# Second-layer weight blocks decoded at other places, kept in device memory in between, in a spectral convolution with two gated MLPs

## The chip, the cores and the metric

The kernel runs on one core of one Trainium2 chip. The metric is the device time of one execution in microseconds (us), the median of several runs. The profiled execution is one more execution, taken with the hardware profiler.

## What is computed

Activations, two filter arrays and five weight arrays come in; the weights are double precision. A spectral convolution over 3008 positions (2 batches, 256 channels) is followed by two MLPs over the 6016 tokens that result. Cut to what matters:

```python
def _attn_ref(x, filt_r, filt_i):              # x: (2, 3008, 256)
    X = np.fft.rfft(x, axis=1)
    Y = X * (filt_r + 1j * filt_i)[None]
    return np.fft.irfft(Y, n=x.shape[1], axis=1)

def _moe_ref(x, w_gate, w_val, w_out):         # 256 -> 1536 -> 256
    gate = 1.0 / (1.0 + np.exp(-(x @ w_gate)))
    return gate * (x @ w_val) @ w_out

def _moe2_ref(x, w_in, w_out):                 # 256 -> 2048 -> 256
    h = x @ w_in
    return h * (1.0 / (1.0 + np.exp(-1.702 * h))) @ w_out
```

## The kernel before

**Precision.** Every operand of TensorE is a pair of float32 tiles, a high part (rounded by a ScalarE copy) and a low part (the rest, a subtraction on VectorE or GpSimd). `mm3` (L119) makes one product out of three matmuls, high by high, high by low and low by high (L120, L121, L122). The weights arrive as double-precision bits, in blocks of 128 x 512 values. One block is decoded on VectorE and ScalarE: two mask operations, three combining ones, a high copy, a low subtraction. For the first layer this is `decode_steps` (L152), for the second `decode_chores` (L1048).

**Stages.** The tokens are in 12 tiles of up to 512 (the last two of each batch have 480). First comes the convolution of batch 0 (to about 65 us of the trace). Then a first pass of the first MLP layer over tiles 0 to 3 (`s12`, to 187 us) runs while the first layer's 18 weight blocks are decoded, about three for every two steps `f` of the hidden dimension (12 steps of 128). Then the convolution of batch 1 runs interleaved with tiles 2 to 5 (187 to 390 us). Up to here, from the end of the first convolution, the order of instructions on PE, DVE, ACT and POOL is left to the framework; SP's queue follows the program's order throughout.

From about 400 us on, the order on all engines is the program's. Tiles 6 to 11 go in pairs (`for p in range(3, nt // 2)`), and each hidden step of a pair is computed with **seven products instead of eight** (a Strassen-like scheme): `Forms` (L838 to L890) makes the sums and differences of the two input halves, with a high and a low part each, and `combine_w1` those of the weights. The second layer does the same for six pairs of tiles, 8 double steps `fp` each (`for p in range(nt // 2)`); one `fp` is 7 products and 8 back products (`Block.back`) of three matmuls, 45 matmuls.

**Chores.** Work that is not on the way of a step is put into a list of small steps (`chores`), each a few instructions. `spend(q, n)` takes `n` of them at fixed places in each hidden step, and when the list is empty it takes the next second-layer weight block from `bulk`. A block with an odd number (from `w_out`) has 5 steps: `start`, `mant`, `sign`, `value`, `low`. One with an even number (from `w_in`) has 8, since it also makes the sums of its sub-blocks (`sums`, L1092 to L1103). Between two takings the step's own instructions stand: in the second layer L1405 (`y = x + s5`), L1407 (`z = z + s1`) and L1414 (`w = x + s5`) on DVE, the gate (L1334, L1335) twice for each of the four results on ACT, and its low part (L1338) on POOL. TensorE's product 6 overwrites what L1405 reads, so it waits for it.

**Where second-layer weights lie.** There are 16 blocks, two for each `fp`. Blocks 0 to 3 lie in `wl`, 4 to 15 in `wg`, over the first layer's weights, which is why block 4 can't be decoded before the last first-layer pair has passed its step. Before: blocks 0 to 3 are decoded beside pair 4, 4 to 6 beside pair 5, and 7 to 15 beside the first second-layer pair, with 10 chores for each `fp` (`rate = (3, 1, 3, 3)`). `raw_job` loads the next block's bits, `next_raw` those of the first layer's, into `raw` tiles of the `st0`, `st1`, `st3` and later `st2` pools; `slots` lists the free ones.

Of the kernel before, what the change touches and what calls it, by code (L numbers as in the profile page):

```python
# [17 lines left out]
P = 128  # L18
S = 3008
B = 2  # L20
D = 256
# [66 lines left out]
def kernel(  # L88
# [23 lines left out]
    xscr = dram.tile([12, D, 512], F32, name="xscr")  # L112

# [85 lines left out]

    def next_raw():  # L200
        if jobs and slots:
            load_raw(jobs.pop(0))
# [711 lines left out]
    for t in range(2, 6):  # L914
        for f in range(FK if t < 4 else 0, FC1):
# [30 lines left out]
            if pools is not None and k == NCH + 3:  # L946
# [16 lines left out]
                sp = [w34.tile([P, 6, P], F32R, name=f"sp{i}") for i in range(2)]  # L963
# [9 lines left out]
                fs.dst[3] = [packed(w, n) for w in xk]  # L973
# [7 lines left out]
                w2, w3 = lazy(lambda: combos(PRE)), lazy(lambda: combos(PRE + 1))  # L981
                pre = [w2]
                pre += [lambda: (fs.hi(0), fs.hi(1)), lambda: (fs.lo(0), one(), fs.hi(4)), lambda: fs.lo(1)]
                pre += [lambda: (fs.lo(4), two(), fs.hi(5)), lambda: (three(), fs.lo(5)), four]
                pre += [lambda: fs.hi(3), lambda: fs.lo(3), w3]
# [26 lines left out]
    fs.dst[2], fs.dst[6] = ([packed(h[:, c], n) for h in k26] for c in range(2))  # L1012


    NJ = FC2
    KEEP = NWL

    def slot(j):
        if j < KEEP:
            return [w[:, j] for w in wl]  # L1020
        return [w[:, j - KEEP].rearrange("p v c m -> p (v c m)") for w in wg]

    jobs2 = []
    for i in range(0, FC2, 2):
        jobs2.append((rows(w_in2[:, i * P:(i + 2) * P]), 2 * P))
        jobs2.append((rows(w_out2[i * P:(i + 2) * P, :]), D))
# [6 lines left out]
    def spare3(fp):  # L1033
        if fp < 2:
            return [x[:, 3 * fp:3 * fp + 3, :] for x in sp]
        if fp < 6:
            a = 0 if fp < 4 else 8
            b = 3 * (fp % 2)
            return [w[:, a:a + 4, :].rearrange("p f (c m) -> p (f c) m", c=2)[:, b:b + 3, :] for w in wo]
        return [x[:, 24 + 3 * (fp - 6):27 + 3 * (fp - 6), :] for x in sx1]  # L1040

    def spare2(i):
        return [x[:, i % 3, :] for x in spare3(i // 3)]

    def decode_chores(j):
        fp = j // 2
        hi, lo = slot(j)
        sp = spare3(fp)  # L1048
        t = {}

        def start():
            t["raw"], _, _, own = raws.pop(0)
            slots.append(own)
            t["lw"], t["hw"] = t["raw"][:, :, 0], t["raw"][:, :, 1]
            ex = st.tile([P, 512], U32, tag="ex", name="ex")
            nc.vector.tensor_single_scalar(ex, t["hw"], 0x7FF00000, op=ALU.bitwise_and)  # L1056
            t["c"] = st.tile([P, 512], I32, tag="c", name="c")
            nc.scalar.activation(out=t["c"], in_=ex, func=AF.Relu, bias=ebias, scale=8.0)
            t["m"] = st.tile([P, 512], U32, tag="m", name="m")
            nc.vector.tensor_scalar(t["m"], t["hw"], 0xFFFFF, 0x100000, op0=ALU.bitwise_and, op1=ALU.bitwise_or)  # L1060

        def mant():
            t["f"] = t["m"].bitcast(F32)
            nc.vector.scalar_tensor_tensor(  # L1064
                out=t["f"], in0=t["lw"], scalar=2.0**-32, in1=t["m"], op0=ALU.mult, op1=ALU.add
            )

        def sign():
            cu = t["c"].bitcast(U32)
            nc.vector.scalar_tensor_tensor(  # L1070
                out=cu, in0=t["hw"], scalar=0x80000000, in1=cu, op0=ALU.bitwise_and, op1=ALU.bitwise_or
            )
            raw_job(j + 2)

        def value():
            nc.vector.scalar_tensor_tensor(  # L1076
                out=t["f"], in0=t["f"], scalar=2.0**-20, in1=t["c"].bitcast(F32), op0=ALU.mult, op1=ALU.mult
            )
            nc.scalar.activation(out=hi, in_=t["f"], func=AF.Copy)

        def low():
            nc.vector.tensor_sub(lo, t["f"], hi.bitcast(F32))  # L1082
            if j % 2:
                done.add(j)

        def sums(k):
            if k == 0:
                t["v"] = t["f"].rearrange("p (c i m) -> p c i m", c=2, m=P)
                t["r"] = st.tile([P, 4, P], F32, tag="ex", name="wr")
            v, r = t["v"], t["r"]  # L1090
            if k == 0:
                nc.vector.tensor_add(r[:, 0], v[:, 0, 1], v[:, 1, 1])  # L1092
                nc.vector.tensor_sub(r[:, 1], r[:, 0], v[:, 0, 0])
            else:
                nc.vector.tensor_sub(r[:, 2], v[:, 0, 0], v[:, 0, 1])
                nc.vector.tensor_sub(r[:, 3], v[:, 1, 0], r[:, 1])
                nc.scalar.activation(out=hi[:, P:2 * P], in_=r[:, 0], func=AF.Copy)
                nc.scalar.activation(out=sp[0], in_=r[:, 1:], func=AF.Copy)

        def end():  # L1100
            r = t["r"]
            nc.vector.tensor_sub(lo[:, P:2 * P], r[:, 0], hi[:, P:2 * P].bitcast(F32))
            nc.vector.tensor_sub(sp[1], r[:, 1:], sp[0].bitcast(F32))  # L1103
            done.add(j)

        return [start, mant, sign, value] + ([low] if j % 2 else [lambda: sums(0), low, lambda: sums(1), end])

    done = set()
# [13 lines left out]
    def forms_chores(dst, n, raws, spread, split_too):  # L1122
        def make():
            fs = Forms(dst, n, raws, spread, [st.tile([P, 512], F32, tag=k, name="xs") for k in ("ex", "c", "m")])
            cell.append(fs)
            steps = fs.sums()
            if split_too:
                ks = (0, 1, 4, 5, 2, 6, 3)
                steps.append(lambda: fs.hi(0))
                for k, nxt in zip(ks, ks[1:]):  # L1130
                    steps += [lambda k=nxt: fs.hi(k), lambda k=k: fs.lo(k)]
                steps.append(lambda: fs.lo(3))
            return steps

        cell = []
        return lazy(make), cell
# [43 lines left out]

    left = None
    held = []
    low2 = None
    ready = set(range(PRE + 2))
# [11 lines left out]
    for p in range(3, nt // 2):  # L1196
        n = tiles[2 * p][3]
        rhs = [[h[:, :n] for h in d] for d in setA]
        for f in range(FC1):
# [12 lines left out]
            if first_set:  # L1212
                chores += [lazy(lambda q=q: weights(q)) for q in range(PRE + 2, FC1)]
# [5 lines left out]
            if p + 1 < nt // 2:  # L1219
                if f == 9:  # L1220
                    lz, cell = forms_chores(setA, tiles[2 * p + 2][3], raw2, True, False)
                    chores.append(lz)
            elif f == 7:
                lz, cell = forms_chores(setB, 512, raw2, False, True)
                chores.append(lz)
            if p == 3 and f == 10:
                raw_job(0)
                raw_job(1)
            if f == 0:
                bulk += range(4) if p == 4 else ()  # L1230
            if p == 5 and f == 3:
                bulk += range(4, 7)
            rate = {3: (1, 2, 1), 4: (1, 2, 0), 5: (1, 2, 1)}[p]
            if p == 4 and f > 8 or p == 5 and f < 3:
                rate = (0, 0, 0) if not chores else rate
# [10 lines left out]
            if first_set:  # L1246
                fs.hi(6)
                fs.hi(2)
# [14 lines left out]
            if first_set:  # L1263
                fs.lo(6)
# [14 lines left out]
            if first_set:  # L1279
                fs.lo(2)  # L1280
# [5 lines left out]
            if last:  # L1286
                nf.hi(6)
                nf.lo(1, nc.gpsimd)
                nf.lo(6)
# [3 lines left out]
            if last:  # L1293
# [15 lines left out]
            if last:  # L1309

                def low2(nf=nf):
                    nf.hi(3)
                    nf.lo(2)
# [12 lines left out]
    class Block:  # L1326
        def __init__(self, i, j, p, fp, bank):
            self.i, self.j, self.t, self.fp, self.bank = i, j, 2 * p + j, fp, bank
            self.n = tiles[self.t][3]

        def act(self):
            self.gp = [x[:, :self.n] for x in gslot()]
            self.sg = work.tile([P, 512], F32, tag="sg", name="sg")[:, :self.n]
# [3 lines left out]
        def low(self):  # L1337
            nc.gpsimd.tensor_sub(self.gp[1], self.sg, self.gp[0].bitcast(F32))  # L1338
# [21 lines left out]

    for p in range(nt // 2):
# [3 lines left out]
        for fp in range(FC2 // 2):  # L1365
# [4 lines left out]
            if fp == 0:  # L1370
                bulk += range(7, NJ) if p == 0 else ()
                while p and chores:
                    chore(chores)
            while 2 * fp + 1 not in done:
                spend(chores, 1)
# [7 lines left out]
            if not asked and (fp >= 3 if p else fp >= 4 and not bulk and not chores or fp == 6):  # L1383
                asked = True
                lz, cell = forms_chores(setA if p % 2 == 0 else setB, tiles[2 * p + 2][3], raw2, False, True)
                chores.append(lz)
            rate = (2, 0, 1, 1) if p else (3, 1, 3, 3) if fp else (0, 0, 0, 3)
# [6 lines left out]
            if left:  # L1394
                for step in left:
                    step()
                left = None
            back()
# [4 lines left out]
            spend(chores, rate[0])  # L1403
# [5 lines left out]
            bz.low()  # L1409
            back()  # L1410
            back()
            spend(chores, rate[1])
            prod(x, 6, False)
            nc.vector.tensor_add(w, x, s5[:, :n])  # L1414
# [59 lines left out]
```

## Time and profile before

| | us |
|---|---|
| median of 3 runs | 1184.28 (1182.04 to 1185.79) |
| the profiled execution's own time | 1183.55 |
| its span, first to last instruction | 1181.7 |
| PE busy in the span | 1149.4 (97%) |
| DVE busy | 696.4 (59%) |
| ACT busy | 674.7 (57%) |
| POOL busy | 480.3 (41%) |

A matmul of 128 x 512 takes about 0.39 us by its record, but the next one starts 0.227 us after it; 20 us in which TensorE never waits hold 90 of them. So the count of matmuls in a stretch tells more than the busy share.

### The profile page before, as it was taken

The numbers are of one execution on the slowest core, as the hardware profiler recorded it, in microseconds if no ns is written. First come the engines' busy times: TensorE is split into PE (matmuls) and PEld (weight loads), VectorE is DVE, ScalarE is ACT, GpSimd is POOL, SyncE is SP. The second block draws the span as 40 slices with busy tenths as digits, with TensorE's granted clock in tenths as the row PEclk, the third lists the DMA queues.
The fourth block names the chain that finished last, engine by engine and source line by source line (L and its number), as shares of the span: only waits on it lengthen the run. The fifth ranks groups of instructions, "written<-read, shape, count | busy, mean of one in ns | idle before, by whom it ended". The sixth has DMA issues, their size and how long they took to land.

```text
span 1181.7 us, 14171 instructions
## 1 busy us (share of the span) xinstructions
PE 1149.4 (97%) x4994; PEld 933.3 (79%) x4994; DVE 696.4 (59%) x1149; ACT 674.7 (57%) x1274; POOL 480.3 (41%) x385
## 2 busy tenths in 40 slices
PE   8999999999999899999999988899999999999998
PEld 4468888888888788788888866788888888888887
DVE  6899965465564877877778799843333323233211
ACT  5656644665653555655555655566556556556554
POOL 3910104666663211211211244455555555545443
PEclk9999999999999999999999999899999999999999
DMA  8565502232302200012012033020020100200000
GB/s 199 154 189 176 128 1 75 61 92 67 94 14 81 69 21 1 25 48 72 1 54 72 1 96 101 1 72 1 1 72 1 48 22 1 72 1 1 36 1 34
DMA packets 36007, 66.51 MB, mean 56 GB/s; under 512 B 3648, under 2 KB 12480, under 8 KB 35936
## 3 DMA queue, kind: packets, MB, share of 16 engines
q1 hardware_dynamic: 33968, 62.45, 18.0%
q10 hardware_dynamic: 1968, 3.17, 0.8%
q8 instruction: 39, 0.64, 0.2%
q14 instruction: 32, 0.26, 0.1%
HBM read 45.02 MB, written 19.79 MB: 55 GB/s over the span
## 4 chain that ended last, share of the span: by engine, by line
PE 81%; DVE 10%; DMA 3%; ACT 3%; issue 2%; POOL 1%; SPq 0%; ACTq 0%; DVEq 0%; POOLq 0%
PE ps L120 27%; PE ps L121 27%; PE ps L122 27%; DMA f<-in_fd_dram 2%; DVE c L1070 1%; DVE ex L1056 1%; DVE wg L1082 1%; POOL y L341 1%; DVE m L1076 1%; DVE yp L843 1%; DVE m L1064 1%; DMA yraw<-yscr 0%; POOL v L337 0%; DMA yraw<-tt 0%; DVE m L1060 0%
## 5 line engine op out<-in xcount | busy, mean ns | idle before, releaser
L1338 POOL TENSOR_TENSOR g<-sg,g 128x512 fp32r<-128x512 f32 (+1 forms) x128 | 169.4, 1338 | 168.7 <-ACT sg L1335 163.1
L117 POOL TENSOR_TENSOR g<-sg,g 128x512 fp32r<-128x512 f32 (+1 forms) x80 | 102.2, 1277 | 311.3 <-ACT g L116 297.9
L120 PE MATMUL ps<-yp,wg 128*128 128x512 f32 (+1 forms) x442 | 171.9, 389 | 1.0 <-ACT wg L177 0.8
L121 PE MATMUL ps<-yp,wg 128*128 128x512 f32 (+1 forms) x442 | 170.9, 387 | 0.8 <-DVE yp L117 0.8
L122 PE MATMUL ps<-yp,wg 128*128 128x512 f32 (+1 forms) x442 | 170.4, 386 | 0.0
L1405 DVE TENSOR_TENSOR ps<-ps,tabs 128x512 f32<-128x512 f32 (+1 forms) x48 | 33.0, 688 | 198.8 <-PE ps L122 198.7
L1334 ACT ACTIVATE g<-ps 128x512 fp32r<-128x512 f32 (+1 forms) x128 | 75.9, 593 | 85.8 <-DVE ps L1407 58.0
L1338 POOL TENSOR_TENSOR wo<-sg,wo 128x512 fp32r<-128x512 f32 (+1 forms) x64 | 85.8, 1352 | 78.6 <-ACT sg L1335 74.7
L1335 ACT ACTIVATE sg<-ps 128x512 f32<-128x512 f32 (+1 forms) x192 | 114.1, 594 | 3.3 <-POOL g L1338 1.8
L120 PE MATMUL ps<-g,wo 128*128 128x512 f32 (+1 forms) x288 | 111.3, 386 | 0.4 <-ACT wo L177 0.4
L121 PE MATMUL ps<-g,wo 128*128 128x512 f32 (+1 forms) x288 | 111.3, 386 | 0.4 <-POOL g L117 0.4
L122 PE MATMUL ps<-g,wo 128*128 128x512 f32 (+1 forms) x288 | 111.0, 386 | 0.0
L120 PEld LDWEIGHTS ps<-yp,wg 128*128 128x128 f32 x442 | 83.0, 188 | 18.3 <-ACT wg L177 1.2
L121 PEld LDWEIGHTS ps<-yp,wg 128*128 128x128 f32 x442 | 83.0, 188 | 16.6 <-issue 1.7
L122 PEld LDWEIGHTS ps<-yp,wg 128*128 128x128 f32 x442 | 82.9, 188 | 16.0
L116 ACT ACTIVATE g<-sg 128x512 fp32r<-128x512 f32 (+1 forms) x80 | 49.6, 620 | 55.7 <-DVE sg L464 30.4
L120 PE MATMUL ps<-g,wg 128*128 128x512 f32 (+1 forms) x192 | 74.0, 386 | 0.0
L122 PE MATMUL ps<-g,wg 128*128 128x512 f32 (+1 forms) x192 | 74.0, 386 | 0.0
L121 PE MATMUL ps<-g,wg 128*128 128x512 f32 (+1 forms) x192 | 74.0, 386 | 0.0
L1414 DVE TENSOR_TENSOR ps<-ps,tabs 128x512 f32<-128x512 f32 (+1 forms) x48 | 33.0, 688 | 56.5 <-PE ps L122 56.5
L120 PEld LDWEIGHTS ps<-g,wo 128*128 128x128 f32 x288 | 54.1, 188 | 11.9 <-ACT wo L177 0.8
L1334 ACT ACTIVATE wo<-ps 128x512 fp32r<-128x512 f32 (+1 forms) x64 | 38.0, 594 | 44.4 <-DVE ps L1407 31.1
(290 smaller groups left out, 2770.6 us busy)
## 6 DMA issues: line engine op xcount, KB each, us to landing
yraw<-xscr SPq DMA_DIRECT2D x16, 512.0 KB, 4.4
raw<-in_w_out_dram SPq DMA_DIRECT2D x14, 512.0 KB, 3.9
x<-in_xd_dram SPq DMA_DIRECT2D x15, 384.0 KB, 5.3
yraw<-yscr SPq DMA_DIRECT2D x11, 512.0 KB, 5.3
yscr<-tt SPq DMA_DIRECT2D x40, 128.0 KB, 2.1
xscr<-yraw SPq DMA_DIRECT2D x10, 512.0 KB, 2.8
f<-in_fd_dram SPq DMA_DIRECT2D x23, 192.0 KB, 4.4
raw<-in_w_in_dram SPq DMA_DIRECT2D x8, 512.0 KB, 3.8
```

What stands on the lines that cost most here:

```text
L116: nc.scalar.activation(out=dst_hi, in_=src, func=AF.Copy)
L117: lo_eng.tensor_sub(dst_lo, src, dst_hi.bitcast(F32))
L120: nc.tensor.matmul(out=o, lhsT=w[0], rhs=x[0], start=first, stop=False, **kw)
L121: nc.tensor.matmul(out=o, lhsT=w[0], rhs=x[1], start=False, stop=False, **kw)
L122: nc.tensor.matmul(out=o, lhsT=w[1], rhs=x[0], start=False, stop=last, **kw)
L341: eng.tensor_add(y, y, v)
L843: (eng or nc.vector).tensor_sub(self.dst[k][1], self.src[k], self.dst[k][0].bitcast(F32))
L1334: nc.scalar.activation(out=self.gp[0], in_=self.bank, func=AF.Gelu_apprx_sigmoid)
L1335: nc.scalar.activation(out=self.sg, in_=self.bank, func=AF.Gelu_apprx_sigmoid)
L1338: nc.gpsimd.tensor_sub(self.gp[1], self.sg, self.gp[0].bitcast(F32))
L1405: nc.vector.tensor_add(y, x, s5[:, :n])
L1414: nc.vector.tensor_add(w, x, s5[:, :n])
```

## The change

It does the following.

- Blocks 0 to 3 are appended to `jobs`, so that their bits are loaded and decoded in the first pass (`decode_next`), behind the first layer's 18 blocks. Their high and low parts go into one place, tiles of `st1` (`early_place`), and from there to a new tensor in device memory (`wscr`; the sums to `sscr`). `st1` gets no more raw bits from then on.
- Blocks 4 to 15 are in `bulk` from the start of pair 4; blocks 4 to 11 are decoded into `wl` in turn (`j % NWL`) and stored to `wscr`, 12 to 15 stay there. Blocks below 12 are loaded into `wg[j]` (`reload`) once the last first-layer pair has passed step j; the sums are loaded by `reload_s` into `wo`, `sx0` and `sx1`.
- The numbers of chores taken change: `RATE` and the lines behind it for the first layer, with `hold_back` at the end of pairs 4 and 5; `(0, 0, 0)` for the first `fp` and `(3, 2, 2)` for the others of the first second-layer pair, at three places instead of four. `spend` stops ahead of a `low` or `end` step unless it is the first that it takes.
- Two inputs of the first-layer pairs (numbers 2 and 6) get tiles of their own (`ks`, `kr`), so that some high and low copies are made earlier instead of in the pair's first or last step. `w3` is combined inside pair 3.
- In the first `fp` of the first second-layer pair, the first block keeps its gate result in PSUM and makes its low part on DVE, one place later (`own`).

The core of the diff:

```diff
+    wscr = dram.tile([FC1, 2, P, 512], F32, name="wscr")
+    sscr = dram.tile([FC2 // 2 - 1, 2, P, 3 * P], F32, name="sscr")
...
+        def spill():
+            done.add(j)
+            if j < KEEP:
+                for i, x in enumerate((hi, lo)):
+                    nc.sync.dma_start(out=wscr[j, i], in_=x.bitcast(F32))
+            if j % 2 == 0 and fp < 7:
+                for i, x in enumerate(sp):
+                    nc.sync.dma_start(out=sscr[fp, i], in_=x.rearrange("p k m -> p (k m)").bitcast(F32))
...
+    KEEP = FC1
+    EARLY = 4
+    jobs += [(j, [jobs2[j][0]], jobs2[j][1]) for j in range(EARLY)]
+
+    def early_place():
+        own = stage[1]
+        w = own.tile([P, 2, 512], F32R, tag="raw", name="wl0")
+        return [w[:, 0], w[:, 1]] + [own.tile([P, 3, P], F32R, tag=k, name="sp0") for k in ("c", "m")]
...
             if raws and (t == 0 or f % 2 == 1):
-                decode(nc.vector)
+                decode_next()
                 next_raw()
     while raws:
-        decode(nc.vector)
+        decode_next()
...
+                kr = st2.tile([P, 2, 512], F32R, tag="raw", name="kr", bufs=2)
+                fs.dst[2], fs.dst[3], fs.dst[6] = ([packed(w, n) for w in k] for k in (ks, xk, kr))
...
+    def reload(j):
+        placed.add(j)
+        for i, x in enumerate(slot(j)):
+            nc.sync.dma_start(out=x.bitcast(F32), in_=wscr[j, i])
...
+    RATE = {3: (1, 2, 2), 4: (1, 2, 1), 5: (1, 2, 1)}
+    SPARE = (4, 0), (5, 1), (11, 5)
...
     def spend(q, n):
-        for _ in range(n):
-            if not q and bulk:
-                q.extend(decode_chores(bulk.pop(0)))
+        for k in range(n):
+            if not q and bulk and not hold_back:
+                q.extend(next_decode(bulk.pop(0)))
+            if k and q and getattr(q[0], "apart", False):
+                return
             chore(q)
...
+                raw_job(EARLY)
+            if p == 4 and f == 0:
+                raw_job(EARLY + 1)
+                bulk += range(EARLY, NJ)
+            hold_back = p == 4 and f > 7 or p == 5 and f > 6
+            rate = RATE[p] if p == 3 or f > 2 else (0, 2, 1) if f else (0, 0, 1)
+            if p == 5:
+                for q in range(FC1):
+                    if q < f and q in done and q not in placed:
+                        reload(q)
+                for q, g in SPARE:
+                    if f >= q and 2 * g in done and g not in summed:
+                        reload_s(g)
...
+            if p == 0:
+                for g in (0, 1, 4, 5, 6, 2, 3):
+                    if (fp or g not in (2, 3)) and 2 * g in done and g not in summed:
+                        reload_s(g)
+                for q in range(FC1):
+                    if q in done and q not in placed:
+                        reload(q)
+                while 2 * fp + 1 not in done:
+                    spend(chores, 1)
...
-            rate = (2, 0, 1, 1) if p else (3, 1, 3, 3) if fp else (0, 0, 0, 3)
+            rate = (2, 1, 1) if p else (3, 2, 2) if fp else (0, 0, 0)
```

## Rows read from the trace of the kernel before

**Rows 1.** The page: span, busy time by engine, PE in 40 slices.

```profile
span 1181.7 us, 14171 instructions
...
PE 1149.4 (97%) x4994; PEld 933.3 (79%) x4994; DVE 696.4 (59%) x1149; ACT 674.7 (57%) x1274; POOL 480.3 (41%) x385
...
PE   8999999999999899999999988899999999999998
```

**Rows 2.** Windows (stretch, busy by engine, granted clock, DMA): second-layer pairs 0, 1.

```profile
674.00:775.00 101.00, 88.31 (x355) 68.42 (x354) 89.19 (x118) 61.42 (x117) 48.32 (x34) 0.95 0.18 58
774.00:856.00 82.00, 82.00 (x363) 67.94 (x362) 26.27 (x39) 47.60 (x89) 42.30 (x32) 1.00 0.08 26
```

**Rows 3.** Timeline of DVE (start, duration): L1405 of second-layer pairs 0, 1, 2.

```profile
674.51 0.69 DVE L1405 TENSOR_TENSOR ps<-ps,tabs 128x512 f32<-128x512 f32 x1
...
774.30 0.70 DVE L1405 TENSOR_TENSOR ps<-ps,tabs 128x512 f32<-128x512 f32 x1
...
776.95 0.70 DVE L1414 TENSOR_TENSOR ps<-ps,tabs 128x512 f32<-128x512 f32 x1 [1.34 <-PE ps L122]
...
855.86 0.67 DVE L1405 TENSOR_TENSOR ps<-ps,tabs 128x480 f32<-128x480 f32 x1 [6.81 <-PE ps L122]
```

**Rows 4.** Waits of PE, 674 to 775 us: total, times, longest.

```profile
PE ps L120 <- DVE ps L1405: 5.2, 5, 2.3
PE ps L120 <- ACT s L1393: 4.3, 4, 3.3
```

**Rows 5.** Groups on DVE, 674 to 775 us (count, busy, mean ns): block decoding.

```profile
L1070 DVE SCALAR_TENSOR_TENSOR c<-raw,c 128x512 uint32<-128x512 uint32 x9 | 10.4, 1155 | 0.0
...
L1060 DVE TENSOR_SCALAR m<-raw 128x512 uint32<-128x512 uint32 x9 | 4.9, 548 | 0.0
L1092 DVE TENSOR_TENSOR wr<-m 128x128 f32<-128x128 f32 x4 | 3.1, 782 | 0.1
...
L1103 DVE TENSOR_TENSOR sx<-wr,sx 128x384 fp32r<-128x384 f32 x2 | 1.1, 553 | 0.4 <-ACT sx L1098 0.4
```

**Rows 6.** Timeline of DVE: the two own adds between which nine chores stand.

```profile
714.07 0.69 DVE L1414 TENSOR_TENSOR ps<-ps,tabs 128x512 f32<-128x512 f32 x1
...
725.50 0.69 DVE L1405 TENSOR_TENSOR ps<-ps,tabs 128x512 f32<-128x512 f32 x1
```

**Rows 7.** Windows: last step of second-layer pair 0; first-layer pair 5.

```profile
760.00:780.00 20.00, 20.00 (x90) 16.57 (x89) 14.97 (x16) 13.68 (x27) 11.94 (x8) 1.00 0.00 1
640.00:660.00 20.00, 20.00 (x94) 17.31 (x93) 15.12 (x28) 11.70 (x23) 3.66 (x3) 1.00 0.01 1
```

**Rows 8.** Windows: starts of first-layer pairs 3 and 4.

```profile
400.00:420.00 20.00, 17.36 (x73) 13.17 (x73) 16.93 (x38) 12.05 (x28) 3.87 (x4) 1.00 0.39 131
480.00:500.00 20.00, 18.29 (x78) 14.03 (x76) 17.47 (x27) 12.72 (x23) 5.26 (x4) 1.00 0.01 5
```

**Rows 9.** Windows: first pass with decoding, and its end without.

```profile
80.00:153.00 73.00, 72.81 (x322) 59.99 (x321) 70.25 (x125) 46.13 (x82) 4.76 (x4) 1.00 0.50 148
153.00:187.00 34.00, 34.00 (x151) 27.90 (x150) 18.22 (x33) 12.59 (x25) 3.28 (x3) 1.00 0.04 16
```

**Rows 10.** Groups on DVE, 80 to 160 us: decoding beside an idle POOL.

```profile
L167 DVE SCALAR_TENSOR_TENSOR c<-raw,c 128x512 uint32<-128x512 uint32 x15 | 11.1, 738 | 1.6 <-ACT c L159 1.6
...
L161 DVE TENSOR_SCALAR m<-raw 128x512 uint32<-128x512 uint32 x14 | 5.7, 418 | 0.0
```

**Rows 11.** Timeline of DVE: the last low part of a first-layer block.

```profile
152.86 0.69 DVE L180 TENSOR_TENSOR wg<-m,wg 128x512 fp32r<-128x512 f32 x1
```

**Rows 12.** Timeline of PE: the first matmul of the second convolution.

```profile
187.31 0.40 PE L120 MATMUL ps<-xp,tab 96*128 96x512 f32 x1
```

**Rows 13.** Timeline of SP's queue: loads of the second convolution.

```profile
126.09 0.41 SPq L228 DMA_DIRECT2D x<-in_xd_dram  x1
```

**Rows 14.** The page, DMA issues (count, KB each, us to landing).

```profile
x<-in_xd_dram SPq DMA_DIRECT2D x15, 384.0 KB, 5.3
...
xscr<-yraw SPq DMA_DIRECT2D x10, 512.0 KB, 2.8
```

More of the change, by code (lines that the diff above doesn't have):

```diff
@@ new lines, with decode_next @@
+    NJ = FC2
+    KEEP = FC1
+    EARLY = 4
+    done = set()
+    jobs += [(j, [jobs2[j][0]], jobs2[j][1]) for j in range(EARLY)]
[3 more added lines that the diff above has]
+        return [w[:, 0], w[:, 1]] + [own.tile([P, 3, P], F32R, tag=k, name="sp0") for k in ("c", "m")]
+    def decode_next():
+        if isinstance(raws[0][1], int):
+            early = early_place()
+            j = raws[0][1]
+            for step in decode_chores(j, raws[0][3], lambda: (early[0], early[1], early[2:])):
+                step()
+        else:
+            decode(nc.vector)
@@ L1033, in spare3 @@
     def spare3(fp):
[L1034 to L1040, printed above, removed]
-    def spare2(i):
[L1043 to L1106, printed above, removed]
@@ new lines, with reload_s @@
+    placed = set(range(KEEP, NJ))
+    summed = {7}
+    def reload(j):
+        assert j in done, j
+        placed.add(j)
+        for i, x in enumerate(slot(j)):
+            nc.sync.dma_start(out=x.bitcast(F32), in_=wscr[j, i])
+    def reload_s(fp):
+        assert 2 * fp in done, fp
+        summed.add(fp)
+        for i, x in enumerate(spare3(fp)):
+            k = 0
+            for v in x:
+                nc.sync.dma_start(
+                    out=v.bitcast(F32), in_=sscr[fp, i, :, k * P:(k + v.shape[1]) * P].rearrange("p (k m) -> p k m", m=P)
+                )
+                k += v.shape[1]
@@ L1125, in make @@
             cell.append(fs)
-            steps = fs.sums()
-            if split_too:
+            one, two, three, four = fs.sums()
+            if len(ahead) == 7:
                 ks = (0, 1, 4, 5, 2, 6, 3)
-                steps.append(lambda: fs.hi(0))
+                steps = [one, two, three, four, lambda: fs.hi(0)]
                 for k, nxt in zip(ks, ks[1:]):
                     steps += [lambda k=nxt: fs.hi(k), lambda k=k: fs.lo(k)]
-                steps.append(lambda: fs.lo(3))
-            return steps
+                return steps + [lambda: fs.lo(3)]
+            steps = [one, three]
+            for k in ahead:
+                steps += [lambda k=k: fs.hi(k), lambda k=k: fs.lo(k)]
+            return steps + [two, four]
         cell = []
@@ L1197 @@
         n = tiles[2 * p][3]
-        rhs = [[h[:, :n] for h in d] for d in setA]
+        rhs = [[h[:, :n] for h in d] for d in sets[p]]
         for f in range(FC1):
@@ L1292 @@
             nc.scalar.activation(out=sgy, in_=y, func=AF.Sigmoid)
-            if last:
+            if last and 2 not in AHEAD[p]:
                 nf.hi(2)
@@ L1329, in __init__ @@
             self.n = tiles[self.t][3]
+            self.own = p == 0 and i == 0
         def act(self):
             self.gp = [x[:, :self.n] for x in gslot()]
[L1333 removed]
+            self.sg = self.bank if self.own else work.tile([P, 512], F32, tag="sg", name="sg")[:, :self.n]
             nc.scalar.activation(out=self.gp[0], in_=self.bank, func=AF.Gelu_apprx_sigmoid)
@@ L1412 @@
             spend(chores, rate[1])
+            if not bz.own:
+                bz.low()
             prod(x, 6, False)
             nc.vector.tensor_add(w, x, s5[:, :n])
+            if bz.own:
+                bz.low()
             bw.act()
```

157 lines of the change are left out of this document (106 added, 51 removed).

## The prediction

> **What bounds the kernel now.** I read the page first: TensorE is busy 97% of the span, so little is to be had from anything but the places where it waits, and its 40 slices show one such place besides the ends, slices 24 to 26 (680 to 768 us) [rows 1]. The windows say what stands there: the first second-layer pair. It has the same 360 matmuls (8 steps x 45) as the second one, yet its stretch of 101 us shows 355 of them where the next 82 us show 363; VectorE (DVE) is busy 89.2 us of the 101, against 26.3 of 82 [rows 2]. The length of a pair is read from its opening add, L1405: pair 0 lasts 774.30 - 674.51 = 99.8 us, pair 1 lasts 855.86 - 774.30 = 81.6 us, 10.2 us for each step [rows 3]. So pair 0 loses **18.2 us**, the largest loss in the kernel. What ends the waits is DVE's L1405, and ScalarE behind it [rows 4]; they are only the first of what is missing, since the granted clock also falls there, to a mean of 0.95 [rows 2].
>
> The groups show what DVE does meanwhile: nine blocks are decoded, six operations each, 46.1 us in all (the six rows between the first two of [rows 5], counts 9), so 5.12 us a block; the four even ones add seven rows of sums, 16.0 us in all, 4.0 us a block [rows 5]. That is 62.1 us for 5 x 5 + 4 x 8 = 57 chores, 1.09 us a chore. Ten chores and 2.1 us of own adds make about 13 us a step, more than the 10.2 that TensorE needs. Where they hurt is seen in one step: from L1414 to the next L1405 three takings of three chores stand in DVE's queue, and the gap is 725.50 - 714.07 = 11.4 us [rows 6]; without them TensorE sets a gap of 784.5 - 776.95 = 7.5 us (the next step of pair 1 opens 10.2 us after 774.30) [rows 3].
>
> **The second-layer pair.** I counted the chores through the code's lists. Blocks 0 to 3 are done in the first pass; beside pairs 4 and 5 stand seven blocks as before, now 4 to 10; so five remain (11 to 15, three odd, two even), 31 chores in steps 1 to 5, six or seven a step and none in step 0. Block 15 is finished in step 5, needed in step 7; nothing is forced. DVE loses four blocks, 4 x 5.12 + 2 x 4.0 = 28.5 us, and has 89.2 - 28.5 = 60.7 us left for 81.6 us. Between L1414 and L1405 there are now at most 2 + 3 chores, 5.5 us at 1.09, less than the 7.5. Steps 6 and 7 hold seven chores for the next pair's inputs; before, with ten, step 7 ran with 90 matmuls in 20 us while DVE was busy 15.0 [rows 7]. The whole 18.2 us could go; I leave 2 us for chores that meet GpSimd (POOL) three times in a row: **16.2 us gained**, between 8 (below) and 18.2. What is late next is TensorE itself. The low part moved from POOL to DVE in step 0 costs one operation of 0.69 us [rows 3] where no chore stands: nothing, and 0.7 if the next add waited for it.
>
> **The first-layer pairs.** Their waits are at the starts: 20 us with 73 matmuls and 20 with 78 instead of 90 [rows 8], so 17 x 0.227 = 3.9 and 12 x 0.227 = 2.7 us. Two high and low copies are taken out of each of these places, not all that stands there: **2 us gained**, between 0 and 6.6. In pair 3 a step takes 5 chores instead of 4, in pairs 4 and 5 up to 4 where it was 3 or 4. They are costed at nothing: with 4 chores a step DVE was busy 15.1 of 20 us and TensorE had its full 94 matmuls of 480 columns [rows 7]. If that cover went, a step of six own adds (0.69 each) and 4 chores at 1.09 would need 8.5 us where 33 matmuls take 7.5, 1 us for each of some five steps, 5 us lost. The load of block 4 now waits on SP's queue for a tile that pair 3 reads to its end; only block 5's bits and pair 3's results are queued behind it, and the first chore of block 4 comes at the last place of the next step: nothing.
>
> **Stores and loads.** Twelve blocks and seven sets of sums go out and come back, each store on SP waiting for a block's last DVE step and each load for TensorE to have passed that step of `wg`. Behind such a wait on SP stand the next blocks' bits, the next inputs, asked for a step ahead, and the other loads. A store of 512 KB landed in 2.8 us [rows 14], and every block is loaded at least one step of 7 us or more before its use, so it costs nothing; if a load came a whole step late, 7 to 10 us, once.
>
> **The first pass.** Here DVE is full: 70.3 of 73 us until 153, while TensorE lacks nothing worth naming [rows 9]; the last first-layer block ends at 152.86 + 0.69 [rows 11]. From there to 187 DVE is busy only 18.2 of 34 us [rows 9], free 15.8. Beside an idle POOL a block's six operations take 3.75 us (the means of the rows between the first and last of [rows 10], which are L167 and L161). Four blocks are 15 us, the sums of two some 4 us more at the duration of their shortest operations: 19 us into 15.8, with about 5 us of weight sums and table work done there that can wait. So decoding just ends as the second convolution starts, whose first matmul is at 187.31 [rows 12]. Its loads were issued at 126 [rows 13]; in SP's order they now stand behind the last block's stores, at about 183. A load lands in 5.3 us [rows 14], the split of x takes some 2 us, so the convolution's first matmul comes near 192, 5 us late. TensorE has first-layer steps to do meanwhile, which need nothing of it, but later runs out of them sooner. I take **2.5 us lost**, between 0 and 6.
>
> **The sum** against the profiled execution: 1183.55 - 16.2 - 2.0 + 2.5 = 1167.9. The median stands 0.7 above that execution, so 1168.6; forecast 1168.5.
>
> **Rivals.** *Lock* (chance 0.15): in pair 0 chores are longer than in the first pass: 1155 and 548 ns against 738 and 418 [rows 5, 10]. If each of POOL's 42.3 us [rows 2] held up a chore, DVE would need the 26.3 us of pair 1 [rows 2], five blocks at 3.75 with 4 us of sums, and 42.3: 91.4 us for the pair, a gain of 8.4 and 1176.5. For it speak those durations; against it step 7, full with ten chores [rows 7]. The Trainium skill, "SBUF — State Buffer", Who interferes with whom, says that the port pair of VectorE and GpSimd is an exclusive lock: a VectorE operation with two SBUF inputs waits for a whole GpSimd one that reads SBUF. By it this rival's bound would be the rule; the means in both groups agree in kind, as L1405, with one input in PSUM, stays at 0.69 beside them.
>
> *One place* (0.08, slower): the four early blocks share one place, so block j + 1's high copy on ScalarE waits until block j's stores have landed. Behind it in ScalarE's queue stand the gates of the running steps, and only two steps (8 us) are in flight. An even block has four stores, some 5 us from its last subtraction to landing (2.8 [rows 14] and the issues); three reuses are 15 us, with the 6 us of a late convolution 21 us. Against a gain of 18.2 that gives 1184.3 + 21 - 18.2 = 1187. It decides from 18.2 us on; below that the order, which the framework makes with the waits in view, puts other work ahead, and TensorE has shown no wait with DVE at 96% [rows 9].
>
> *Late loads* (0.07): the stores and loads don't free the pair, since one block comes back late on SP: 8 us of the gain go, 1176.5.
>
> **How the numbers follow.** Forecast 0.65 (1160 to 1174), lock 0.15, late loads 0.07, one place 0.08, and 0.05 that these add up to no change. A measurement of this kernel tells from no change only what is over 0.3%, 3.6 us. Faster: 0.65 + 0.15 + 0.07 = 0.87; same 0.05; slower 0.08. The low end takes all that pair 0 and the starts lose, 18.2 + 6.6, with nothing lost in the first pass: 1159.5, so 1160. The high end takes in the lock and the late loads with 3 us more: 1180. That leaves out some 0.15.
>
> **What would show it.** Right: pair 0 of the second layer from L1405 to L1405 near 83 us, DVE busy some 60 us in it, clock 1.00; the windows at the pairs' starts with a few matmuls more; a wait of TensorE near the second convolution's start of a few us. Wrong: pair 0 at 90 us or more with chores still at 1.1 us or longer, ScalarE waiting for stores between 155 and 190 us, or fewer than 90 matmuls in 20 us anywhere in the first pass.

## The result

The changed kernel takes **1162.64 us** in the median (1161.39 to 1164.87, 6 runs), the kernel before 1183.48 (1182.04 to 1185.79, 6 runs); the ratio is 0.9826, 95% interval 0.9812 to 0.984. That is 20.8 us less; the forecast was 1168.5, 15.7 less, in a range of 1160 to 1180. The profiled execution took 1163.64 us, 19.9 less than the one before.

The page after answers to [rows 1]: the 8 of slices 24 to 26 is gone.

```profile
span 1161.8 us, 14340 instructions
...
PE 1142.4 (98%) x4994; PEld 930.3 (80%) x4994; DVE 683.0 (59%) x1165; ACT 670.9 (58%) x1274; POOL 449.6 (39%) x369
...
PE   8999999999999999999999999999999999999998
```

The windows of the first two second-layer pairs (stretch, then busy us and count of PE, PEld, DVE, ACT, POOL, granted clock, DMA) answer to [rows 2]. Pair 0 now shows 357 matmuls in 84 us at full clock, DVE busy 64.9 us and POOL only 22.5 instead of 48.3.

```profile
671.00:755.00 84.00, 82.27 (x357) 66.04 (x356) 64.87 (x96) 55.55 (x104) 22.47 (x17) 1.00 0.23 76
755.00:837.00 82.00, 82.00 (x364) 67.95 (x363) 26.98 (x38) 46.99 (x89) 41.37 (x32) 1.00 0.08 26
```

TensorE's clock had a small part in pair 0's old length. The granted clock of 0.95 over its 101 us [rows 2] is some 10 us at half speed (1.2 instead of 2.4 GHz), in two dips. The step with the first takes 12.8 us, no more than the two behind it, which have none, so there TensorE didn't set the time. The second reaches into the pair's seventh step, which has one decoding operation left and takes 12.4 us instead of 10.2. So by estimate some 2 of the 16.6 us below are the clock. This dip follows 3 us in which TensorE shows 4 matmuls:

```profile
746.00:749.00 3.00, 0.76 (x4) 0.30 (x2) 2.58 (x6) 0.75 (x2) 0.78 (x1) 1.00 0.00 0
749.00:756.00 7.00, 5.98 (x14) 4.72 (x15) 4.05 (x7) 3.17 (x6) 1.12 (x1) 0.52 0.00 0
```

The timeline of DVE with the adds that open pairs 0, 1 and 2 (L1483 is the L1405 of before) answers to [rows 3]: 754.98 - 671.81 = **83.2 us** for pair 0 where it was 99.8, and still 81.6 for pair 1.

```profile
671.81 0.70 DVE L1483 TENSOR_TENSOR ps<-ps,tabs 128x512 f32<-128x512 f32 x1 [1.03 <-PE ps L124]
...
754.98 0.70 DVE L1483 TENSOR_TENSOR ps<-ps,tabs 128x512 f32<-128x512 f32 x1 [0.61 <-PE ps L124]
...
836.54 0.67 DVE L1483 TENSOR_TENSOR ps<-ps,tabs 128x480 f32<-128x480 f32 x1 [6.82 <-PE ps L124]
```

Where the 19.9 us came from, between marks that both traces hold (PE's matmuls by their start, pairs by their first add on DVE):

| stretch | before, us | after, us | difference |
|---|---|---|---|
| start to the first first-layer matmul | 57.58 | 57.31 | -0.3 |
| first pass, to the second convolution's first matmul | 129.73 | 129.04 | -0.7 |
| second convolution, first to last matmul | 184.81 | 187.66 | +2.9 |
| from there to first-layer pair 3 | 31.70 | 29.67 | -2.0 |
| first-layer pair 3 | 92.62 | 91.50 | -1.1 |
| pair 4 | 91.13 | 89.91 | -1.2 |
| pair 5 | 86.94 | 86.72 | -0.2 |
| second-layer pair 0 | 99.79 | 83.17 | -16.6 |
| pair 1 to the end | 407.4 | 406.8 | -0.6 |

The first line varies with the first loads from run to run, from 56.6 to 59.6 us in the runs below; the others repeat within 0.2 us in kernels with the same code there, except the first pass of the kernel before (129.7 and 132.6) and the second convolution after the change (186.1 to 187.7, and 188.9 once, told below). So a stretch tells what a total doesn't.

### The profile page after: what moved, and what is told of

Its sections match the earlier page's. It is cut to its first block, busy times and chain, and to the rows that moved or that the text cites. A ratio compares the mean times of both kernels' runs of the same rounds, so it can differ in the third digit from the quotient of the medians.

```text
span 1161.8 us, 14340 instructions
## 1 busy us (share of the span) xinstructions
PE 1142.4 (98%) x4994; PEld 930.3 (80%) x4994; DVE 683.0 (59%) x1165; ACT 670.9 (58%) x1274; POOL 449.6 (39%) x369
## 4 chain that ended last, share of the span: by engine, by line
PE 85%; DVE 6%; ACT 3%; issue 2%; DMA 2%; POOL 1%; SPq 0%; ACTq 0%; DVEq 0%; POOLq 0%
PE ps L122 28%; PE ps L123 28%; PE ps L124 28%; DMA x<-in_xd_dram 1%; DMA yraw<-yscr 1%; DMA f<-in_fd_dram 0%; POOL y L443 0%; DVE yp L945 0%; PE ps L449 0%; ACT g L118 0%; PE ps L411 0%; DVE c L231 0%; PE ps L461 0%; PE ps L421 0%; DVE sg L566 0%
## 5 line engine op out<-in xcount | busy, mean ns | idle before, releaser
L1407 POOL TENSOR_TENSOR g<-sg,g 128x512 fp32r<-128x512 f32 (+1 forms) x117 | 149.5, 1290 | 174.5 <-ACT sg L1404 172.6
L119 POOL TENSOR_TENSOR g<-sg,g 128x512 fp32r<-128x512 f32 (+1 forms) x80 | 102.3, 1279 | 278.5 <-ACT g L118 278.3
L1483 DVE TENSOR_TENSOR ps<-ps,tabs 128x512 f32<-128x512 f32 (+1 forms) x48 | 33.0, 688 | 220.1 <-PE ps L124 217.4
L1407 POOL TENSOR_TENSOR wo<-sg,wo 128x512 fp32r<-128x512 f32 (+1 forms) x59 | 75.5, 1289 | 84.9 <-ACT sg L1404 84.2
L1404 ACT ACTIVATE sg<-ps 128x512 f32<-128x512 f32 (+1 forms) x176 | 104.7, 595 | 1.0 <-POOL g L1407 0.8
L122 PEld LDWEIGHTS ps<-g,wo 128*128 128x128 f32 x288 | 54.1, 188 | 11.9 <-ACT wo L179 0.8
L123 PEld LDWEIGHTS ps<-g,wo 128*128 128x128 f32 x288 | 54.1, 188 | 11.8 <-POOL g L119 1.0
```

Source lines behind the costliest of these rows:

```text
L119: lo_eng.tensor_sub(dst_lo, src, dst_hi.bitcast(F32))
L122: nc.tensor.matmul(out=o, lhsT=w[0], rhs=x[0], start=first, stop=False, **kw)
L123: nc.tensor.matmul(out=o, lhsT=w[0], rhs=x[1], start=False, stop=False, **kw)
L1404: nc.scalar.activation(out=self.sg, in_=self.bank, func=AF.Gelu_apprx_sigmoid)
L1407: (nc.vector if self.own else nc.gpsimd).tensor_sub(self.gp[1], self.sg, self.gp[0].bitcast(F32))
L1483: nc.vector.tensor_add(y, x, s5[:, :n])
```

## The experiments

Each was compared with the kernel before on the same chip; "the pair" is second-layer pair 0 from first add to first add.

**All low parts on POOL.** The text ahead of the prediction says that only the first block of the first step makes its low part on DVE. The code says more: `own` holds for two of the four blocks in all eight steps of the pair, 16 operations, which explains POOL's 22.5 us. This run takes them back:

```diff
-            self.own = p == 0 and i == 0
+            self.own = False
```

> The changed kernel, with the low parts of the first second-layer pair all back on GpSimd (in the change 16 of its 32 are made on VectorE). Theory 'count' (what VectorE has to do in the pair sets its length): VectorE loses 16 operations of 0.69 us, 11 us, the pair stays at 82 to 84 us (83.2 in the changed kernel), 1162 to 1164 us in all. Theory 'lock' (chores are long because they meet GpSimd): GpSimd goes from 22 to about 42 us in the pair, the chores get longer, the pair lasts 88 to 91 us, 1168 to 1171 us in all.

Measured: the pair 81.85 us, 1163.18 us in all (1161.71 to 1164.6), ratio 0.9813 (0.9797 to 0.983). The windows of the pair:

```profile
671.00:755.00 84.00, 83.08 (x362) 67.20 (x361) 65.44 (x81) 55.41 (x105) 47.05 (x33) 1.00 0.22 76
```

"Count" has the time right and its reason only half. DVE lost 16 operations and is as busy as with them (65.4 us), for the chores grew: the same operation of a block in the groups on DVE, first after the change, then here (count, busy, mean ns):

```profile
L221 DVE TENSOR_SCALAR m<-raw 128x512 uint32<-128x512 uint32 x5 | 4.3, 859 | 0.0
```

The same group with the low parts on POOL:

```profile
L221 DVE TENSOR_SCALAR m<-raw 128x512 uint32<-128x512 uint32 x5 | 5.5, 1094 | 0.0
```

The busy times of a block's six operations add up to 30.3 us for five blocks here, 6.1 a block, and to 25.2 after the change, 5.0 a block. "Lock" is right that chores lengthen and wrong that the pair does: TensorE isn't waiting for the chores' end. On the contrary the pair is 1.3 us shorter, so the 16 low parts on DVE cost something. The waits after the change show what it most likely is: a low part stands in DVE's queue until ScalarE has made its gate (us in total, times, longest), and TensorE waits for low parts in its turn; with all of them on POOL neither wait is there.

```profile
DVE g L1407 <- ACT ps L1404: 5.9, 5, 1.6
...
DVE wo L1407 <- ACT ps L1404: 2.6, 3, 1.5
...
PEld ps L122 <- DVE g L1407: 1.6, 2, 0.8
```

**Ten chores a step.** The five blocks were to stand closer together, at the places of the change, and without the rule of `spend` below:

```diff
-            rate = (2, 1, 1) if p else (3, 2, 2) if fp else (0, 0, 0)
+            rate = (2, 1, 1) if p else (3, 3, 4) if fp else (0, 0, 0)
...
-            if k and q and getattr(q[0], "apart", False):
-                return
```

> The changed kernel, with ten chores a step in the first second-layer pair instead of up to seven, as in the kernel before, at the places of the changed one. The same five blocks are decoded, only closer together. Theory 'count': VectorE has 65 us of work for 82 us in either case, the pair stays at 83 to 85 us, 1163 to 1165 us in all. Theory 'spacing' (each step is as long as the chores taken in it): 31 chores fall into three steps of 2.1 + 1.4 + 10 x 1.09 = 14.4 us instead of 10.2, the pair lasts about 95 us, 1174 us in all.

Measured: the pair 84.56 us, 1167.08 us in all (1165.37 to 1169.21). It isn't the test that was meant. Without the rule, `spend` takes more in pairs 4 and 5 as well: they decode nine blocks instead of seven, and only three are left for this pair, as the group of one operation per block shows (count, busy, mean ns; five after the change, above).

```profile
L221 DVE TENSOR_SCALAR m<-raw 128x512 uint32<-128x512 uint32 x3 | 1.3, 422 | 0.0
```

So there is one full step, with 12 decoding operations on DVE; it took 14.0 us, as "spacing" has it. The next two took 10.6 and 10.2 us with six and none. With the rule alone taken away (below) the pair is 82.8 us, also with three blocks, so the full step costs 1.7 us and part of its delay is made up behind it. Which of the two theories holds for five blocks stays open. Of the longer total, 2.5 us lie in the first-layer pairs 4 and 5, as in that run.

**The low parts on DVE, in the kernel before.** Nothing else of the change:

```diff
+            self.own = p == 0 and i == 0
...
-            self.sg = work.tile([P, 512], F32, tag="sg", name="sg")[:, :self.n]
+            self.sg = self.bank if self.own else work.tile([P, 512], F32, tag="sg", name="sg")[:, :self.n]
...
-            nc.gpsimd.tensor_sub(self.gp[1], self.sg, self.gp[0].bitcast(F32))
+            (nc.vector if self.own else nc.gpsimd).tensor_sub(self.gp[1], self.sg, self.gp[0].bitcast(F32))
...
-            bz.low()
+            if not bz.own:
+                bz.low()
...
             nc.vector.tensor_add(w, x, s5[:, :n])
+            if bz.own:
+                bz.low()
```

> The kernel before, with nothing of the change but the 16 low parts of the first second-layer pair made on VectorE, out of PSUM. Theory 'count': VectorE, which already set that pair's length, gets 16 x 0.68 = 11 us more, the pair goes from 99.8 to 108 to 111 us, 1191 to 1195 us in all. Theory 'lock': GpSimd's work in the pair halves, the nine blocks shrink from 62 us towards 42 (six operations at 3.75 us and 2 us of sums for the even ones), the pair falls to about 91 us, 1175 us in all.

Measured: the pair 100.8 us, 1.0 longer, 1186.17 us in all (1184.11 to 1188.58), ratio 1.0007 (0.9996 to 1.0017). Neither came. The groups' sums are 39.3 us for the six operations of nine blocks and 12.1 for the sums, 51.4 instead of 62.1 [rows 5], 10.7 us less, and the 16 low parts are 10.9 us more. The windows show POOL's load halved and TensorE where it was:

```profile
678.00:779.00 101.00, 86.75 (x350) 67.94 (x349) 84.26 (x132) 62.05 (x117) 22.97 (x17) 0.95 0.18 58
```

DVE is even busy 4.9 us less than before in the same 101 us (84.3 for 89.2 [rows 2]; the next pair's inputs take less too), and the pair is no shorter, so DVE's total alone doesn't set it. TensorE waits less for the add on DVE (1.8 us for 5.2 [rows 4]) and more for ScalarE's copy of s (9.1 for 4.3):

```profile
PE ps L120 <- ACT s L1394: 9.1, 5, 2.5
...
PE ps L120 <- DVE ps L1406: 1.8, 1, 1.8
```

Why ScalarE is later was not tried. This edit of the change is no part of its gain.

**Two early blocks instead of four.** Seven blocks are left for the pair, at up to ten chores a step:

```diff
-    EARLY = 4
+    EARLY = 2
...
-            rate = (2, 1, 1) if p else (3, 2, 2) if fp else (0, 0, 0)
+            rate = (2, 1, 1) if p else (4, 3, 3) if fp else (0, 0, 0)
```

> The changed kernel with only two blocks decoded in the first pass; seven are left for the first second-layer pair, which takes up to ten chores a step for them, from its step 1 to step 6. Theory 'number of blocks': VectorE has 65 + 2 x 5.0 + 4 = 79 us for 82 us in that pair, five steps take 12 us or more instead of 10.2, the pair lasts 88 to 93 us, 1167 to 1172 us in all; the second convolution's stretch shrinks by up to 2 us. Theory 'places' (the pair was long for where its chores stood and not for their number): the pair stays at 83 to 85 us, 1160 to 1163 us in all.

Measured: the pair **90.06 us**, 1168.09 us in all (1167.0 to 1168.84), ratio 0.9867 (0.9851 to 0.9882); the second convolution's stretch 184.96. "Number of blocks" holds: nine, seven and five blocks give 99.8, 90.1 and 83.2 us, three give 82.8 (the run without the rule, below), and TensorE's own time is 81.6. The number of chores a step rises with the blocks, so the two aren't told apart here. Of the 9.7 us between nine and seven some 2 are the clock, which is 1.00 in this run. In the window DVE is busy 73.9 of 90 us and TensorE is 44 matmuls short of the 397 that 90 us hold:

```profile
670.00:760.00 90.00, 82.82 (x353) 64.88 (x352) 73.94 (x113) 57.35 (x109) 23.14 (x17) 1.00 0.34 114
```

**No copies ahead.** Input 2's copies back in the last step of pairs 3 and 4:

```diff
-    AHEAD = {3: (2,), 4: (2,), 5: ()}
+    AHEAD = {3: (), 4: (), 5: ()}
```

> The changed kernel, with the high and low copies of input 2 made in the last step of first-layer pairs 3 and 4 again, not ahead of it. If these copies stood in TensorE's way at the pairs' starts, pairs 3 and 4 (91.5 and 89.9 us from first add to first add in the changed kernel) go back towards 92.6 and 91.1, 1 to 2.5 us in all, 1164 to 1165 us. If the earlier gain of these pairs came from the chores' new places alone, nothing changes: 1162 to 1163 us.

Measured: pair 3 92.2 us, pair 4 89.9, pair 5 86.2, 1162.73 us in all (1162.32 to 1165.39). The copies ahead are worth 0.7 us in pair 3 and nothing in pair 4, and pair 5 is 0.6 us longer with them (86.7): at both borders the last step of a pair is 0.6 us shorter and the first of the next one 0.5 to 0.6 longer. Over the three pairs they are worth 0.1 us.

**Without the rule of `spend`.** A `low` or `end` step may stand right behind the step whose high copy it needs:

```diff
-            if k and q and getattr(q[0], "apart", False):
-                return
```

> The changed kernel without the rule that a low or end step is only taken first, so that more chores stand together. If VectorE waiting in its queue for ScalarE's high copy (the instruction right ahead of a low step) is what costs, first-layer pairs 4 and 5 go from 89.9 and 86.7 us to 91 and 87.5 or more and the second-layer pair 0 from 83.2 to 84 or more, 1165 us in all. If only the number of chores counts, all stay within 0.3 us, 1162 to 1163 us in all.

Measured: pair 4 91.3 us, pair 5 87.8, the second-layer pair 82.8, 1164.81 us in all (1162.9 to 1166.83; the profiled execution's second convolution took 188.9 us, with a granted clock of 0.95 from 187 to 220 us). Pairs 4 and 5 are 1.4 + 1.1 = 2.5 us longer, the second-layer pair 0.4 shorter. But the rule also breaks takings off, and without it pairs 4 and 5 decode nine blocks instead of seven, the second-layer pair three instead of five. First the group of one operation per block in pairs 4 and 5, after the change:

```profile
L221 DVE TENSOR_SCALAR m<-raw 128x512 uint32<-128x512 uint32 x7 | 2.9, 420 | 0.0
```

And in this run:

```profile
L221 DVE TENSOR_SCALAR m<-raw 128x512 uint32<-128x512 uint32 x9 | 3.8, 421 | 0.0
```

So neither expectation is decided: the 2.5 us are the price of the missing rule and of two more blocks together. The waits of DVE and of PE's weight loads from pair 4 to the second layer (us in total, times, longest) say where TensorE lost them. In its timeline each of the five waits of the weight loads for an add (L1348) stands right behind a wait of DVE for ScalarE, four times in a `low` or `end` step and once in a low part of an input.

```profile
DVE wl L243 <- ACT wl L240: 1.4, 2, 0.7
...
PEld ps L122 <- DVE ps L1348: 3.1, 5, 0.7
```

After the change the longest wait of PE's weight loads in these pairs is another and small:

```profile
PEld ps L122 <- ACT s L1317: 0.3, 1, 0.3
```

**The weight sums of step 3 ahead again.**

```diff
+                pre += [lazy(lambda: combos(PRE + 1))]
...
-    ready = set(range(PRE + 1))
+    ready = set(range(PRE + 2))
...
-                chores += [lazy(lambda q=q: weights(q)) for q in range(PRE + 1, FC1)]
+                chores += [lazy(lambda q=q: weights(q)) for q in range(PRE + 2, FC1)]
```

> The changed kernel with the weight sums of step 3 made ahead of pair 3 again, as in the kernel before. From the second convolution's last matmul to pair 3's first add the changed kernel takes 29.7 us, the kernel before 31.7. If those sums, in front of the pair on VectorE, cost the 2 us, it goes back to 31 or more, 1164 to 1165 us in all. If the early copies of inputs 2 and 6 won them, it stays under 30.2, 1162 to 1163 us in all.

Measured: 404.67 - 373.37 = 31.3 us from the second convolution's last matmul to pair 3's first add, against 403.68 - 374.01 = 29.7 after the change; 1163.96 us in all (1163.09 to 1167.09). So 1.6 of the 2.0 us there come from these sums being moved into pair 3, which gives 0.4 back (91.1 here, 91.5 after). The timelines of PE (the last matmul) and DVE (the add, L1335 here) in this run, where a whole-weight sum, L894, stands right ahead of the add:

```profile
373.37 0.42 PE L124 MATMUL ps<-zp,tab 128*96 128x512 f32 x1
...
404.06 0.68 DVE L894 TENSOR_TENSOR wex<-wg,wg 128x512 f32<-128x512 f32 x1
404.67 0.68 DVE L1335 TENSOR_TENSOR ps<-ps,tabs 128x512 f32<-128x512 f32 x1
```

The same two after the change, where the add waits for nothing but TensorE:

```profile
374.01 0.42 PE L124 MATMUL ps<-zp,tab 128*96 128x512 f32 x1
...
403.68 0.70 DVE L1334 TENSOR_TENSOR ps<-ps,tabs 128x512 f32<-128x512 f32 x1 [1.64 <-PE ps L124]
```

**Two places for the early blocks.** The high and low parts of blocks 0 to 3 alternate between two tiles:

```diff
-        w = own.tile([P, 2, 512], F32R, tag="raw", name="wl0")
+        w = own.tile([P, 2, 512], F32R, tag="wl0", name="wl0", bufs=2)
```

> The changed kernel with two places in turn for the high and low parts of the four early blocks, so that no block waits for the stores of the one before. Theory 'one place' (ScalarE's wait for stores delays decoding, and with it the second convolution's loads): decoding ends some 5 us sooner, the convolution's first x is loaded before 172 us (174.75 in the changed kernel), and its stretch from first to last matmul goes back from 187.2 towards 184.8 us, 2 us gained, 1160.5 us in all. Theory 'VectorE sets it' (decoding fills VectorE): nothing moves, loads at 174 to 176, stretch 186 to 187.7 us, 1162 to 1163 us in all.

Measured: the second convolution's stretch 370.96 - 186.12 = **184.8 us**, as before the change; 1160.63 us in all (1160.45 to 1163.43), ratio 0.981 (0.9792 to 0.9828). "One place" holds by the times: in the six runs with one place and four early blocks x is issued 11.6 us ahead of the convolution's first matmul and the stretch is 186.1 to 188.9 us; with two places it is 14.2 us ahead, with two early blocks 22.8, and the stretch is 184.8 to 185.0. SP's queue and ScalarE show it, first after the change, then here. After the change the last block's stores are issued at 172.85 and x at 174.75, and ScalarE waits 3.25 us for that load:

```profile
172.85 1.81 SPq L251 DMA_DIRECT2D wscr<-wl  x2
174.75 0.38 SPq L330 DMA_DIRECT2D x<-in_xd_dram  x1
...
181.69 0.63 ACT L118 ACTIVATE xp<-x 96x512 fp32r<-96x512 f32 x1 [3.25 <-DMA x<-in_xd_dram]
```

With two places the stores are issued at 170.82, x at 171.96, and the wait is 0.17 us:

```profile
170.82 1.05 SPq L251 DMA_DIRECT2D wscr<-wl  x2
171.96 0.39 SPq L330 DMA_DIRECT2D x<-in_xd_dram  x1
...
176.21 0.63 ACT L118 ACTIVATE xp<-x 96x512 fp32r<-96x512 f32 x1 [0.17 <-DMA x<-in_xd_dram]
```

The length of that wait isn't the loss: with two early blocks ScalarE waits 1.88 us for x, earlier, and the stretch loses nothing. The framework also orders ScalarE's and VectorE's work from 158 to 192 us otherwise with two places (the copies of f and the weight sums come sooner); how much of the gain is the earlier load and how much this order was not tried.

**Both edits that gained.** Two places, and all low parts of the second-layer pair on POOL.

```diff
-        w = own.tile([P, 2, 512], F32R, tag="raw", name="wl0")
+        w = own.tile([P, 2, 512], F32R, tag="wl0", name="wl0", bufs=2)
...
-            self.own = p == 0 and i == 0
+            self.own = False
```

> The changed kernel with both edits that gained: two places for the early blocks, and all low parts of the second-layer pair 0 on GpSimd. If the two add up (2.0 us in the second convolution, 1.3 us in that pair), the convolution's stretch is 184.8 us, the pair 81.9 us, and the whole 1159.5 us, 3 us under the changed kernel. If GpSimd's longer work lets the pair stall in this arrangement, the pair is 83 us or more and the whole 1160.5 to 1161.5 us.

Measured: **1158.93 us** (1158.3 to 1161.69, 5 runs), ratio to the kernel before 0.9787 (0.9773 to 0.98), below both kernels; the second convolution 184.85 us, the pair 81.7, within 0.2 us of the pairs that decode nothing. The two add up.

```profile
671.00:753.00 82.00, 81.16 (x354) 65.62 (x353) 64.07 (x79) 54.96 (x104) 47.01 (x33) 1.00 0.23 78
```

## Why the prediction was right, point by point

**The second-layer pair**, the term that carried the forecast: 16.2 us foreseen, 16.6 measured. The reason was tested with two early blocks: each of two blocks put back, with the chores a step that they bring, costs 3.4 us ((90.06 - 83.17) / 2), and from seven to the nine of the kernel before, whose other edits are missing too, it is 4.9 each, some 1 of it the clock. Two points of the step were wrong, and that the sum came out is in part luck. DVE was to be left with 60.7 us; it had 64.9, 10.9 of them 16 low parts where one was reckoned with (the misreading told above). But without them it has 65.4, since a block's six operations then take 6.1 us and not the 5.12 of [rows 5]. And the 2 us left for chores that meet POOL are not lost there: 1.6 us stay lost, 1.3 of them with those low parts on DVE.

**The first-layer pairs**: 2.0 us foreseen, 2.0 + 2.6 measured, inside the bound of 6.6. The term was under-sized and its reason mostly another one. I put the gain on the copies of inputs 2 and 6. Input 2's in the pairs' last steps are worth 0.1 us in all; those taken out of pair 3's first step were not tried by themselves. The sums of step 3 moved into pair 3 are worth 1.6, of which pair 3 pays 0.4. A third piece is read from the traces and was not tried: in the kernel before, the first chore of block 0 stands ahead of the add that opens pair 4 (1.8 us from its start to that add), and pair 3's last step takes 10.3 us; after the change it takes 7.9, and 8.5 without the copies ahead. First before, then after:

```profile
494.67 1.51 DVE L1056 TENSOR_SCALAR ex<-raw 128x512 uint32<-128x512 uint32 x1
496.10 0.42 DVE L1060 TENSOR_SCALAR m<-raw 128x512 uint32<-128x512 uint32 x1
496.44 0.69 DVE L1267 TENSOR_TENSOR ps<-ps,tabs 128x512 f32<-128x512 f32 x1
```

```profile
494.57 0.69 DVE L1374 TENSOR_TENSOR g<-ps,g 128x512 fp32r<-128x512 f32 x1 [1.06 <-ACT g L1371]
495.18 0.69 DVE L1334 TENSOR_TENSOR ps<-ps,tabs 128x512 f32<-128x512 f32 x1
```

The prediction costed the chores' new places and numbers at nothing: it took 4 a step as harmless because pair 5 had run with 4 at 94 matmuls in 20 us [rows 7], and did not ask what an in-order queue does where a chore stands ahead of a pair's first add or waits for another engine. The rule of `spend` keeps pairs 4 and 5 from losing 2.5 us, together with the two blocks that it keeps out of them.

**The first pass**: 2.5 us lost foreseen, 2.9 lost in the second convolution and 0.7 or more won ahead of it. The mechanism was right: the convolution's loads stand behind the last block's stores on SP. Their time was not: I had decoding end at 183, and it ended at 174, with the last low part at 173.63 (x issued at 174.75); DVE had more room than the 15.8 us that I counted, since the weight sums and the table were put behind the blocks and the first layer's last low part was made at 149.15 instead of 152.86. The convolution's first matmul wasn't late (186.35, before 187.31); the loss is behind it, with 79 matmuls from 175 to 195 us where the kernel before has 91. That 2.5 came so near is luck in part: the six executions of this code lost 1.2 to 4.0 us there, the most with the clock at 0.95. And the rival *one place* was no rival to the gain but a part of this term, at these 1 to 4 us instead of 21. Of the waits for stores that it reckoned with, and that the prediction named as a sign of being wrong, ScalarE shows one of 1.03 us, at 177.30, ahead of a table's copy.

**What I had not foreseen** is a gain ahead of the second convolution. In the kernel before ScalarE, in the middle of decoding, waits for the convolution's filter, whose load was issued at 126 already; in one execution 1.7 us, in another 4.6, and the first pass was 129.7 and 132.6 us long. After the change it was 129.0 in every run, for those loads come later. The waits of ScalarE from 120 to 160 us in the kernel before:

```profile
ACT f L282 <- DMA f<-in_fd_dram: 1.7, 1, 1.7
```

And in the kernel before with the low parts on DVE, whose first pass is the same code:

```profile
ACT f L282 <- DMA f<-in_fd_dram: 4.6, 1, 4.6
```

That these waits made the whole difference was not tried by itself; TensorE's waits for a VectorE result behind them were 0.2 and 2.6 us in the two first passes, and none after the change.

**The rivals.** *Lock* fell: with POOL's load back at 47 us the blocks were a fifth longer and the pair 1.3 us shorter. The lengthening itself agrees with what the Trainium skill says in "SBUF — State Buffer", Who interferes with whom, of the exclusive lock on the port pair that VectorE and GpSimd share: a block's six operations take 3.75 us with POOL idle, 5.0 with POOL busy 22 us of the pair and 6.1 with 47. *Late loads* didn't happen: no step of the pair waits for a reload, and none of its PE waits is on a DMA.

**The sum.** Against the profiled execution 15.7 us were foreseen and 19.9 measured: 2.6 us more from the first-layer pairs and their start, 0.6 from start, first pass and second convolution together (1.9 lost, not 2.5), 0.4 from the pair, 0.6 at the end. The other 1.7 us to the median are the 0.7 that I added and the 1.0 by which the profiled execution after the change lies above its median.

## What to carry to other kernels

Where a chore list feeds an in-order engine, count in each stage what the engine has to do against the bottleneck's time there; work moved to a stage with room is won (3.4 us for each block here, 4.9 where TensorE's clock fell too) until the rest fits under the bottleneck's time, and no further: with five blocks the pair was within 2 us of it, with three hardly nearer. Then look at what stands behind each chore in the queue: TensorE's waits were found right behind steps that waited for another engine (that taking them first is the cure was not shown apart from the number of blocks), and a second place for blocks that are stored away took the second convolution back to its old length. Count what an experiment really moved: a rule that was to set an order had changed the number of blocks in three pairs. And an edit inside a change that does two things at once (here the low parts on DVE) should be tried alone, even where the whole gains.

## What the runs showed of the hardware that I had not expected

VectorE's second mask operation on 128 x 512 takes 0.42 us beside a nearly idle GpSimd ([rows 10], L161) and 1.1 us on average beside GpSimd's subtractions (L221 above), and yet moving half of these subtractions to VectorE did not pay: VectorE was busy 4.9 us less in 101, and the pair was 1.0 us longer. The second convolution lost 1.2 to 4.0 us when its first load was issued 11.6 us ahead of its first matmul, nothing at 14.2 us, and regained none of it in 185 us.
